# The place of one weight sum in VectorE's order, in a kernel of cosine attention and eight experts

## The chip, the cores and the metric

The kernel runs on one core of one Trainium2 chip. The metric is the device time of one execution in microseconds (us), as the median of several runs. A core has five engines with queues of their own: TensorE (PE in the profile, its weight loads PEld), VectorE (DVE), ScalarE (ACT), GpSimd (POOL) and SyncE (SP). Each works through its own queue in order. In this kernel POOL issues the loads of the inputs and weights, and SP issues the stores of the result and the saves and reloads of some sums.

## The reference

What is computed, cut to what matters:

```python
# attention: q, k, v are (8, 8, 576, 64); phi weights relu(x) with cos and sin of the position
kv = np.einsum('bhsf,bhsd->bhfd', k_p, v)
num = np.einsum('bhsf,bhfd->bhsd', q_p, kv)
den = np.einsum('bhsf,bhf->bhs', q_p, z)[..., None] + 1e-06
x = (num / den) as (4608, 512)

# experts: w1 is (8, 512, 1024), w2 is (8, 1024, 512)
P = np.exp(x @ w_gate - max)          # (4608, 8), then 8 rounds of row and column scaling
for e in range(8):
    h = np.maximum(x @ w1[e], 0.0)
    ye = h @ w2[e]
    out += P[:, e:e + 1] * ye
```

## The kernel before, in words

The kernel has two stages. The first, up to about 190 us, computes the attention into xT (fp16, held in SBUF), and beside it runs expert 0 on the token blocks that are already there. The second stage runs experts 1 to 7 on all 4608 tokens.

In the second stage every product of two matrices is cut into 2 x 2 blocks and done with seven block products instead of eight, after Strassen and Winograd. That takes sums of the operands' blocks ahead of the products and leaves sums of the results behind them.

- The tokens are two halves of 2304. A *unit* is 384 tokens of each half; there are six per expert, n = 0 to 5. Since the xT sums of a unit (S1, S2, S4) are the same for each expert, they are computed once, saved to DRAM by SP and read again for each expert (`x_again`).
- The first layer of a unit is four *groups*, i = 0 to 3 (`group`). A group multiplies with the banks h_ps, copied_ps (Y) and p_ps (Z). ScalarE writes part of the hidden values H through ReLU; VectorE writes the rest through `add_relu`, L600, one fused instruction that adds a saved partial result to the bank p_ps and applies ReLU. There is one bank p_ps, so the next product in it waits for L600. The last product of a group and its add are put off into the next group (`late`).
- The second layer works on pairs of 128 tokens (`Pair.step`, products P1 to P7). Its products go into the three banks rows_ps and into copied_ps, its sums of H are L678, and its accumulations into the result acc_lo and acc_hi are L666. The steps of a unit's pairs are queued in `stream` and woven by `pair_fill` between the first layer's products of the following unit.
- The sums of the weights are done on VectorE in place or into small tiles. `w1_sums` makes those of the first layer for one group (L583 to L586). `w2_first` makes the first of the second layer (L724): it overwrites the upper right block b12 of w2 by b12 - b11. The others (V2, V3, V4, at L689, L690 and L698) are made in the step P1 or P7 of the expert's first pair.
- The weights of expert e + 1 go into the buffer that expert e - 1 leaves (wA and wB in turn). POOL issues the load of w1 when unit 0 of expert e has been written out in the program, and that of w2 behind unit 2 (`load_w1`, `load_w2`, L116 and L122). A load is held until the last reader of the old weights is done.

In the program text, `w2_first(w_next)` is called once ahead of the loop over experts for expert 1, and then in unit 5 of each expert but the last, behind group 0, for the next expert. `w1_sums` for the next expert follow behind groups 1 to 3.

The order on an engine is not always that of the text. A scheduler places the instructions at compile time: in its own model of the time, each engine takes, of the instructions that are ready, the one that stands earliest in the text. An instruction that is ready while the engine would be idle can so stand far ahead of its place in the text. In the first stage, the kernel forbids that by the class `InOrder`, which ties each instruction to the one before it on its engine by an edge without a semaphore ("written order"). In the second stage only TensorE keeps that wrapper (`te`); `ve` and `se` are replaced by the bare engines, and VectorE's and ScalarE's orders are the scheduler's.

Of the kernel before, what the change touches and what calls it, by code (L numbers as in the profile page):

```python
# [14 lines left out]
ALU = mybir.AluOpType  # L15
# [10 lines left out]
def kernel(  # L26
# [10 lines left out]
    nc = tc.nc  # L37
# [41 lines left out]

    P_tok = const.tile([P, NG, E], FP32, name="P_tok")  # L80

    class InOrder:

        def __init__(self, engine):
# [3 lines left out]
        def __getattr__(self, name):  # L88
            def call(*args, **kwargs):
                i = getattr(self.engine, name)(*args, **kwargs)  # L90
                if self.last is not None:
                    tc.add_manual_dep(
                        i.ins,
                        self.last.ins.name,
                        mybir.DependencyInfo(
                            mybir.DependencyClass.NoSync, mybir.DependencyReason.DATA
                        ),
                        reason="written order",
                    )
                self.last = i  # L100
                return i

            return call
# [66 lines left out]
    with ExitStack() as p1:  # L170
# [15 lines left out]
        def load(b, hk):  # L186
# [22 lines left out]
            out=ident[:], in_=ones_sq[:], pattern=[[-1, P]], compare_op=ALU.is_equal,  # L209
# [6 lines left out]
        for hk in range(HK):  # L216
# [5 lines left out]
            out=wrap[:], in0=gidx[:], scalar1=float(S), scalar2=None, op0=ALU.is_ge  # L222
# [3 lines left out]
            out=sval[:], in0=wrap[:], scalar=-float(S), in1=gidx[:],  # L226
# [21 lines left out]
        with nc.allow_low_precision("sums of zeros and ones"):  # L248
            ve.tensor_reduce(
                out=lo[:], in_=rows[:, :, 1, :], axis=AX.XY, op=ALU.add, negate=True  # L250
# [3 lines left out]
                out=sel[:], in0=rows[:, 0:3, 0, :], in1=rows[:, 0:3, 1, :], op=ALU.add  # L254
            )
        ve.tensor_copy(
            out=spread.rearrange("p j hk hh d -> p (j hk hh) d"),
# [332 lines left out]
    def product(ps, lhs, rhs, start):  # L590

        for kh in range(KH):
# [2 lines left out]
                start=(start and kh == 0), stop=(kh == KH - 1), skip_group_check=True,  # L595
            )

    def add_relu(out, ps, t):

        nc.vector._custom_dve(  # L600
            TENSOR_ADD_SAT, out=out, in0=ps[:, 0:TU], in1=t[:], s0=FP32_MAX, s1=0.0
        )

# [7 lines left out]
    def group(hT, tw, xs, n, i, fill):  # L611
# [21 lines left out]
        fill()  # L633
        product(Z, T3, x_part(1, 0, n), True)
        add_relu(h22, Z, u4)
        fill()
        product(X, b22, s4, False)
# [3 lines left out]
        def last():  # L641
            product(Z, T4, x_part(1, 1, n), False)
            add_relu(h21, Z, u2)
# [77 lines left out]

    def w2_first(w):
        b11, b12 = w[1][:, 0:FH, 0:DH], w[1][:, 0:FH, DH:Dm]
        nc.vector.tensor_tensor(out=b12, in0=b12, in1=b11, op=ALU.subtract)  # L724

    def mark(bank):

# [116 lines left out]

    mark(Y[:])
    w2_first(w_next)
    for e in range(1, E):
        w = w_next
        for n in range(NU):
# [5 lines left out]
            for i in range(FH):  # L855
                group(hT, tws[i], xs, n, i, start_fill if e == 1 and n == 0 else pair_fill)
                if i == 1:

                    xs_next = x_tiles()
                    m = (n + 1) % NU  # L860
                    if e == 1 and m:
                        for _ in x_sums(m, xs_next):
                            pass
                    elif not (e == E - 1 and m == 0):
                        x_again(m, xs_next)

                if e > 1 and n == 0 and i == 0:
                    tws[FH - 1] = w1_sums(w, FH - 1)
                if e + 1 < E and n == NU - 1:
                    if i:  # L870
                        tws[i - 1] = w1_sums(w_next, i - 1)
                    else:
                        w2_first(w_next)
# [48 lines left out]
```

## Time and profile before

| | |
|---|---|
| median of 3 runs | 1050.51 us (1050.51 to 1052.1) |
| time of the profiled execution | 1050.02 us |
| its span, first to last instruction | 1048.3 us |
| mean granted TensorE clock | 0.988 |
| PE busy | 987.3 us, 94% |
| DVE busy | 838.9 us, 80% |
| ACT busy | 555.0 us, 53% |
| POOL busy | 129.6 us, 12% |

How to read it: busy time is that of the engine's own instructions. The table of waits puts each idle time of an engine down to what ended it. The chain is the sequence of work that ended last, followed back from the end. A row of a timeline gives the start and the duration in us, the engine, the line, the operation, what is written and what is read, and in brackets the idle time before it with what ended it. An "x4" at the end means that four like instructions are merged in the row. Line 90 is the helper through which instructions in written order are recorded. A window gives the busy time of each engine within a stretch and, behind POOL, the granted TensorE clock (1.00 is full speed). Names such as S_10585 and hs_10725 are tiles with a buffer number.

### The profile page before, as it was taken

To read this page: it belongs to the slowest core of one execution; us is meant where nothing else is said; L and a number is where in the kernel's file an instruction comes from. 1 tells how busy PE (TensorE), PEld (TensorE's weight loads), DVE (VectorE), ACT (ScalarE), POOL (GpSimd) and SP (SyncE) were. 2 spreads that over 40 slices of the span, in tenths; PEclk is the share of its full clock that TensorE was granted. 3 is DMA by queue.
4 is the path that set the end of the run, shared out by engine and by line. 5 is a ranking of instruction groups with operands and counts; after the bars stand their busy time and mean duration, and the time that the engine had idled before them with its cause. 6 is when DMAs were issued, how large, how long until landed. Compare 5 with 4: busy or idle time off the path is not lost.

```text
span 1048.3 us, 20469 instructions
## 1 busy us (share of the span) xinstructions
PE 987.3 (94%) x7914; PEld 684.5 (65%) x7914; DVE 838.9 (80%) x1898; ACT 555.0 (53%) x1244; POOL 129.6 (12%) x160
## 2 busy tenths in 40 slices
PE   4899999889999989998999989998999899999997
PEld 3455554345777757775777767775777667777775
DVE  6788777568999867886889778887879778888787
ACT  4666665345555545554555545554555445555551
POOL 7623200008950000000000000000000000000000
PEclk9999999999999999999999999999999989999999
DMA  9966501523102321033013311033013311013445
GB/s 166 202 87 90 82 4 46 81 41 69 41 23 63 63 48 46 24 83 67 24 35 74 62 31 41 24 86 64 23 46 63 64 38 32 24 46 94 127 91 122
DMA packets 52530, 66.49 MB, mean 63 GB/s; under 512 B 5584, under 2 KB 44240, under 8 KB 52432
## 3 DMA queue, kind: packets, MB, share of 16 engines
q0 software_dynamic: 28000, 30.94, 19.2%
q1 hardware_dynamic: 24352, 34.11, 11.8%
q8 instruction: 62, 1.02, 0.4%
q14 instruction: 36, 0.29, 0.1%
q10 hardware_dynamic: 80, 0.13, 0.1%
HBM read 83.12 MB, written 12.98 MB: 92 GB/s over the span
## 4 chain that ended last, share of the span: by engine, by line
PE 71%; issue 12%; DVE 8%; DMA 7%; ACT 1%; POOL 1%; POOLq 0%; DVEq 0%
PE rows_ps L90 25%; PE h_ps L90 20%; PE copied_ps L90 8%; PE p_ps L90 8%; DMA w2e<-in_moe_w_dram 6%; PE y_ps L90 5%; PE small_ps L90 4%; DVE acc_lo L666 1%; DVE H L600 1%; DVE k_p L90 1%; DVE acc_hi L666 1%; DMA k_ld<-in_k_dram 1%; DVE q_p L90 1%; DVE den L90 0%; DVE v_aug L90 0%
## 5 line engine op out<-in xcount | busy, mean ns | idle before, releaser
L666 DVE SCALAR_TENSOR_TENSOR acc_lo<-rows_ps,P_tok,acc_lo 128x512 f32<-128x512 f32 (+1 forms) x322 | 205.0, 642 | 82.4 <-PE rows_ps L90 82.4
L90 PEld LDWEIGHTS <-H 128*128 128x128 f16 x2080 | 204.3, 98 | 86.7 <-issue 4.8
L90 PEld LDWEIGHTS <-w1e 128*128 128x128 f16 x1632 | 156.8, 98 | 58.9 <-issue 5.8
L90 PE MATMUL h_ps<-xT,w1e 128*128 128x384 f16 (+1 forms) x624 | 156.3, 353 | 0.0
L638 ACT ACTIVATE H<-h_ps 128x384 f16<-128x384 f32 x168 | 82.7, 492 | 112.8 <-PE h_ps L90 112.8
L619 ACT COPY copied_ps<-h_ps 128x384 f32<-128x384 f32 x168 | 79.0, 470 | 41.8 <-PE h_ps L90 41.7
L629 ACT ACTIVATE H<-copied_ps 128x384 f16<-128x384 f32 x168 | 82.9, 493 | 24.7 <-PE copied_ps L90 24.6
L90 PE MATMUL rows_ps<-w2e,H 128*128 128x256 f16 (+1 forms) x568 | 91.9, 286 | 0.0
L90 PE MATMUL copied_ps<-xT,w1e 128*128 128x384 f16 x336 | 83.9, 332 | 0.0
L90 PE MATMUL copied_ps<-w2e,H 128*128 128x256 f16 x504 | 76.0, 274 | 0.0
L116 POOL DMA_DIRECT2D w1e<-in_moe_w_dram x11 | 8.3, 758 | 483.2 <-DVE T_3_7782 L583 89.4
L666 DVE SCALAR_TENSOR_TENSOR acc_lo<-copied_ps,P_tok,acc_lo 128x256 f32<-128x256 f32 x126 | 60.5, 480 | 1.8 <-PE copied_ps L90 1.3
L666 DVE SCALAR_TENSOR_TENSOR acc_hi<-rows_ps,P_tok,acc_hi 128x512 f32<-128x512 f32 x56 | 41.9, 749 | 19.8 <-PE rows_ps L90 19.0
L692 ACT COPY copied_ps<-rows_ps 128x256 f32<-128x256 f32 x126 | 45.2, 359 | 19.2 <-PE rows_ps L90 19.2
L90 PE MATMUL y_ps<-w2e,hT 128*128 128x512 f16 x224 | 54.3, 380 | 0.0
L783 POOL TENSOR_SCALAR acc_lo<-acc_lo,P_tok 128x512 f32<-128x512 f32 x32 | 53.9, 1701 | 0.5 <-DVE P_tok L759 0.5
L678 DVE TENSOR_TENSOR H<-H 128x512 f16<-128x512 f16 x126 | 53.4, 423 | 0.0
L90 ACT ACTIVATE hT<-h_ps 128x512 f16<-128x512 f32 x56 | 33.7, 602 | 17.6 <-PE h_ps L90 17.3
L90 PE MATMUL small_ps<-ident,q_p 128*128 128x128 f16 x288 | 27.4, 229 | 12.8 <-DVE q_p L90 9.0
L90 DVE TENSOR_TENSOR xT<-small_ps,rb 128x384 f16<-128x384 f32 x64 | 26.3, 453 | 16.1 <-ACT rb L90 14.9
L90 PEld LDWEIGHTS <-hT 128*128 128x128 f16 x224 | 19.5, 98 | 25.9 <-issue 6.2
L90 PEld LDWEIGHTS <-q_p 128*128 128x128 f16 x288 | 20.2, 102 | 24.6 <-DVE q_p L90 11.5
(2429 smaller groups left out, 2035.2 us busy)
## 6 DMA issues: line engine op xcount, KB each, us to landing
out_dram<-acc_lo SPq DMA_DIRECT2D x64, 128.0 KB, 2.4
w1e<-in_moe_w_dram POOLq DMA_DIRECT2D x7, 1024.0 KB, 8.9
w2e<-in_moe_w_dram POOLq DMA_DIRECT2D x7, 1024.0 KB, 9.6
q_ld<-in_q_dram POOLq DMA_DIRECT2D x32, 144.0 KB, 4.4
k_ld<-in_k_dram POOLq DMA_DIRECT2D x32, 144.0 KB, 4.6
v_ld<-in_v_dram POOLq DMA_DIRECT2D x32, 144.0 KB, 4.9
w1e<-in_moe_w_dram POOLq DMA_DIRECT2D x4, 256.0 KB, 7.2
w2e<-in_moe_w_dram POOLq DMA_DIRECT2D x4, 256.0 KB, 6.9
```

What stands on the lines that cost most here:

```text
L90: i = getattr(self.engine, name)(*args, **kwargs)
L116: nc.gpsimd.dma_start(out=w[0][:, :, f0:f1], in_=view[:, :, f0:f1])
L600: nc.vector._custom_dve(TENSOR_ADD_SAT, out=out, in0=ps[:, 0:TU], in1=t[:], s0=FP32_MAX, s1=0.0)
L619: nc.scalar.copy(out=Y[:, 0:TU], in_=X[:, 0:TU])
L629: nc.scalar.activation(out=h11, in_=Y[:, 0:TU], func=AF.Relu)
L638: nc.scalar.activation(out=h12, in_=X[:, 0:TU], func=AF.Relu)
L666: nc.vector.scalar_tensor_tensor(out=a, in0=rows, scalar=P_tok[:, g, self.e : self.e + 1], in1=a, op0=ALU.mult, op1=ALU.add,)
L678: nc.vector.tensor_tensor(out=out_, in0=in0, in1=in1, op=op)
L692: nc.scalar.copy(out=self.W, in_=self.U)
L783: nc.gpsimd.tensor_scalar(out=acc(g), in0=acc(g), scalar1=P_tok[:, g, 0:1], scalar2=None, op0=ALU.mult,)
```

## The change

A helper `not_before(earlier, i)` is taken out of `InOrder`: it adds the edge without a semaphore from an instruction `i` to an earlier one, if there is one. `add_relu` notes its last instruction in `latest`. `w2_first` ties its sum to that instruction. At its calls within the loop, `latest` is the add of the product Z in group 0 of unit 5 of the current expert (h22). At the call ahead of the loop no add_relu has been written, `latest` is None, and no edge is added.

```diff
+    def not_before(earlier, i):
+
+        if earlier is not None:
+            tc.add_manual_dep(
+                i.ins,
+                earlier.ins.name,
+                mybir.DependencyInfo(mybir.DependencyClass.NoSync, mybir.DependencyReason.DATA),
+                reason="written order",
+            )
+
     class InOrder:
...
                 i = getattr(self.engine, name)(*args, **kwargs)
-                if self.last is not None:
-                    tc.add_manual_dep(
-                        i.ins,
-                        self.last.ins.name,
-                        mybir.DependencyInfo(
-                            mybir.DependencyClass.NoSync, mybir.DependencyReason.DATA
-                        ),
-                        reason="written order",
-                    )
+                not_before(self.last, i)
                 self.last = i
                 return i
...
+    latest = None
+
     def add_relu(out, ps, t):
 
-        nc.vector._custom_dve(
+        nonlocal latest
+        latest = nc.vector._custom_dve(
             TENSOR_ADD_SAT, out=out, in0=ps[:, 0:TU], in1=t[:], s0=FP32_MAX, s1=0.0
         )
...
     def w2_first(w):
         b11, b12 = w[1][:, 0:FH, 0:DH], w[1][:, 0:FH, DH:Dm]
-        nc.vector.tensor_tensor(out=b12, in0=b12, in1=b11, op=ALU.subtract)
+        not_before(latest, nc.vector.tensor_tensor(out=b12, in0=b12, in1=b11, op=ALU.subtract))
```

## The prediction

> **What bounds the kernel now.** I read the page's busy shares and chain first, then the table of waits, then the timelines of VectorE and TensorE around one wait, then windows cut at the units of the second stage.
>
> ```profile
> PE 987.3 (94%) x7914; PEld 684.5 (65%) x7914; DVE 838.9 (80%) x1898; ACT 555.0 (53%) x1244; POOL 129.6 (12%) x160
> PE 71%; issue 12%; DVE 8%; DMA 7%; ACT 1%; POOL 1%; POOLq 0%; DVEq 0%
> w2e<-in_moe_w_dram POOLq DMA_DIRECT2D x7, 1024.0 KB, 9.6
> ```
>
> TensorE (PE) is busy for 94% of the span, so it is the bound nearly everywhere. Yet 7% of the chain is DMA, and that is worth following, since a weight load of 9.6 us should hide in a stage of hundreds of us. The chain in order of time, and the table of waits, say where it doesn't:
>
> ```profile
> 827.35 9.70 DMA w2e<-in_moe_w_dram
> 837.68 0.74 DVE acc_lo L666
> 838.94 0.80 PE p_ps L90 x2
> ```
>
> ```profile
> DVE w2e L724 <- DMA w2e<-in_moe_w_dram: 26.2, 7, 4.6
> PE p_ps L90 <- DVE H L600: 25.6, 13, 4.8
> ```
>
> L724 is the first sum of the next expert's second layer weights. VectorE (DVE) stood still for it 7 times, 26.2 us in all, and TensorE stood still for DVE's adds L600 for 25.6 us, almost the same sum. The timelines of DVE, TensorE and POOL show that it is one event:
>
> ```profile
> 832.01 0.42 DVE L678 TENSOR_TENSOR H<-H 128x512 f16<-128x512 f16 x1
> 837.07 0.69 DVE L724 TENSOR_TENSOR w2e<-w2e 128x1024 f16<-128x1024 f16 x1 [4.64 <-DMA w2e<-in_moe_w_dram]
> 837.68 0.74 DVE L666 SCALAR_TENSOR_TENSOR acc_lo<-rows_ps,P_tok,acc_lo 128x512 f32<-128x512 f32 x1
> 838.34 0.55 DVE L600 CUSTOM_DVE_ANT_0 H<-p_ps,u_10851 128x384 f16<-128x384 f32 x1
> ```
>
> ```profile
> 833.52 0.60 PE L90 MATMUL rows_ps<-w2e,H 128*128 128x256 f16 x4
> 838.94 0.80 PE L90 MATMUL p_ps<-xT,T_2_10458 128*128 128x384 f16 x2 [4.82 <-DVE H L600]
> 839.54 1.06 PE L90 MATMUL rows_ps<-V_10766,H 128*128 128x256 f16 x4
> ```
>
> ```profile
> 827.35 0.89 POOL L122 DMA_DIRECT2D w2e<-in_moe_w_dram  x1 [25.44 <-PE rows_ps L90]
> ```
>
> POOL issues the load at 827.35. DVE reaches L724 at 832.4, less than 5 us later, and waits until 837.07. Behind it in DVE's queue stand an accumulation and the add L600 that empties the bank p_ps; TensorE's next product needs that bank and waits 4.82 us. Then TensorE runs slowly: four matmuls of 256 columns take 1.06 us where they took 0.60. The windows give the whole price. Each of the first six rows is the unit of 384 tokens per half in which a load lands, for experts 1 to 6; the seventh is the same unit of expert 7, which loads nothing for a successor.
>
> ```profile
> core 0: us, PE busy (x) PEld busy (x) DVE busy (x) ACT busy (x) POOL busy (x), PEclk, DMA share, GB/s
> 244.45:262.75 18.30, 17.40 (x129) 12.49 (x128) 15.69 (x34) 10.15 (x23) 18.30 (x12) 1.00 0.43 88
> 355.26:380.31 25.05, 20.27 (x143) 14.32 (x141) 17.03 (x37) 10.33 (x23) 0.89 (x1) 0.93 0.37 67
> 471.71:496.80 25.09, 20.18 (x143) 14.32 (x140) 17.12 (x37) 10.33 (x23) 0.89 (x1) 0.93 0.37 65
> 588.21:613.10 24.89, 19.96 (x143) 14.24 (x141) 17.12 (x37) 10.33 (x23) 0.89 (x1) 0.93 0.37 67
> 704.50:729.09 24.59, 20.02 (x143) 14.24 (x141) 17.19 (x37) 10.32 (x23) 0.89 (x1) 0.93 0.38 69
> 820.49:847.03 26.54, 21.47 (x142) 14.78 (x140) 17.17 (x37) 10.33 (x23) 0.89 (x1) 0.87 0.36 64
> 938.44:957.13 18.69, 18.44 (x143) 13.68 (x140) 16.43 (x36) 10.23 (x23) 0.00 (x0) 1.00 0.26 70
> 838.94:844.66 5.72, 5.72 (x23) 3.19 (x23) 2.38 (x5) 1.45 (x3) 0.00 (x0) 0.50 0.16 41
> ```
>
> The last row is the stretch behind the wait: granted clock 0.50 for 5.72 us, so 2.86 us are lost there. 4.82 of idle and 2.86 of slow clock make 7.68, and the unit is 26.54 - 18.69 = 7.85 longer than the clean one. That agrees, so I price each wait by its unit's excess and not by DVE's 4.6 us.
>
> **The change, part by part.** *The wait goes from experts 2 to 6.* The edge puts L724 behind `latest`, the last add_relu written when w2_first is called: group 0 of unit 5 of the same expert. Gain, each unit against 18.69: 6.36 + 6.40 + 6.20 + 5.90 + 7.85 = 32.71. Expert 7's unit is a fair measure, since it runs the same products, pair steps and weight sums, and only lacks load and L724. What is late next in that unit: its remaining 0.41 over a plain unit of 18.28 (below), which I leave in.
>
> *Expert 1's unit.* Here DVE waited less and TensorE only 0.60:
>
> ```profile
> 251.86 0.69 DVE L724 TENSOR_TENSOR w2e<-w2e 128x1024 f16<-128x1024 f16 x1 [1.54 <-DMA w2e<-in_moe_w_dram]
> 253.07 0.48 PE L90 MATMUL p_ps<-xT,T_1_3602 128*128 128x384 f16 x2 [0.60 <-DVE H L600]
> ```
>
> Gain between 0 (the next units are short of DVE time anyway) and 0.60; I take 0.3. The call ahead of the loop finds `latest` empty, so the seventh wait stays:
>
> ```profile
> 204.35 0.69 DVE L724 TENSOR_TENSOR w2e<-w2e 128x1024 f16<-128x1024 f16 x1 [2.58 <-DMA w2e<-in_moe_w_dram]
> ```
>
> *L724 in its new place.* It costs DVE 837.68 - 837.07 = 0.61 us of its queue, once per expert, six times. It is not new work, but it moves from the unit above to unit 5, where the sums of the next expert's first layer weights already stand. The rows: unit 5 of expert 6, a unit of expert 1 that is as full, and an ordinary one; then DVE's adds and TensorE's product around the place.
>
> ```profile
> 901.88:920.16 18.28, 18.28 (x142) 13.70 (x140) 17.79 (x48) 10.23 (x23) 0.00 (x0) 1.00 0.12 35
> 281.19:300.23 19.04, 18.52 (x142) 13.69 (x140) 17.82 (x38) 10.23 (x23) 19.04 (x13) 1.00 0.09 32
> 802.21:820.49 18.28, 18.28 (x142) 13.68 (x140) 14.96 (x34) 10.23 (x23) 0.00 (x0) 1.00 0.46 90
> ```
>
> ```profile
> 904.35 0.56 DVE L600 CUSTOM_DVE_ANT_0 H<-p_ps,u_11628 128x384 f16<-128x384 f32 x1
> 914.24 0.55 DVE L600 CUSTOM_DVE_ANT_0 H<-p_ps,u_11748 128x384 f16<-128x384 f32 x1
> ```
>
> ```profile
> 914.94 0.49 PE L90 MATMUL p_ps<-xT,T_2_10458 128*128 128x384 f16 x2
> ```
>
> L724 will start near 904.8 in this expert, right behind the add of 904.35. DVE is busy for 17.79 of this unit's 18.28 us, so I let its 0.61 be handed on in full. The add of 914.24 would end at 914.24 + 0.61 + 0.55 = 915.40, and TensorE wants its bank at 914.94: about 0.45 of waiting. Bounds: 0 per expert, since unit 5 itself now runs at 18.28 with DVE at 17.79, and 17.79 + 0.61 = 18.40 is only 0.12 over, while the unit behind it is as light as the ordinary one (14.96); and 0.76, from the full unit of expert 1 (19.04 - 18.28 with DVE at 17.82). The nearest row is unit 5 itself, so I go below the middle: 0.2, six times 1.2, with 0 and 4.6 as ends. Queued behind L724 there are accumulations, adds L600 and the weight sums of the next expert.
>
> *Does anything wait for L724 itself?* Its result is first read by the sum of the next expert's first pair,
>
> ```profile
> 939.41 0.68 DVE L689 TENSOR_TENSOR V_12084<-w2e 128x1024 f16<-128x1024 f16 x1
> ```
>
> 34 us behind the new place; and the load landed at 837, 67 us ahead of it. So no new wait on either side: cost 0, covered by these margins. If the cover were gone, the price would be the present wait again.
>
> *Queues.* L724 issues no DMA. POOL's load of w2 waits for the last reader of the old buffer, on TensorE, and stays where that puts it; SP's reloads of x don't depend on it. TensorE's order is written out and unchanged. The helper not_before replaces the same code in InOrder and costs nothing: the same edges. What can move is the scheduler's choice on DVE around the two places; I count that in the ends.
>
> *Sum.* 32.7 + 0.3 - 1.2 = 31.8 us. The profiled execution took 1050.02 (span 1048.3), so it would be 1018.2. The median of the runs is 1050.51, 0.5 above it: forecast 1018.7. About 0.2%, 2 us, is what a measurement here can tell from no change.
>
> **Rivals.**
> *Full units turn dearer.* The scheduler's new order lets unit 5 lose up to the 0.76 of expert 1's full unit: 1018.7 - 1.2 + 4.6 = 1022.1, and a little more with other swaps on DVE. For it: DVE at 17.79 of 18.28. Against: the light unit behind.
>
> *The clock drops in unit 5.* If short waits there made TensorE lose its clock once per expert, at the 2.86 that one slow stretch costs, six of them are 17.2: 1036. Against it: the wait of 0.60 in expert 1 was followed by a product of 0.48 us at full speed, and that unit's granted clock is 1.00, as in the full unit of 19.04. [...]
>
> *Only part of the wait goes.* Something else that depends on the load is drawn early into the free place, and half of the price stays: 1018.7 + 16 = 1035. Against: the other DVE readers of the new weights all stand behind L724 by their data.
>
> *It does nothing.* If `latest` stood early in DVE's order, or the edge were not kept, L724 would stay at 837 and the time at 1050.5. Against: an add of unit 5 can't run ahead of its own product, and that add is the row at 904.35.
>
> *Slower.* DVE's lag in unit 5 grows instead of draining: L724's 0.61 delays the add that frees p_ps, TensorE comes late with its products, and DVE's next instructions wait for these. It decides from 33.0 / 6 = 5.5 us lost per expert, a wait as long as the one removed with its slow clock; at 7 us per expert, 1050.5 - 33.0 + 42 = 1059.5. Against: nine times the instruction's own time, beside a unit with over 3 us of DVE idle.
>
> **How the numbers follow.** Forecast (waits gone, unit 5 hidden or nearly) 72%; dearer full units 13%; clock 4%; part of the wait 4%; nothing 3%; slower 3%; better than my ends 1%. Faster by over 0.2%: 72 + 13 + 4 + 4 + 1 = 94%; within 3%; slower 3%. Low end: 1050.5 - 32.7 - 0.6 = 1017.2, less 1.5 for expert 1's three units, of which the 19.04 is 0.76 over the floor, and for differences between executions: 1015.5. High end: 1022.1 and as much for swaps, 1023.5. Outside lie the clock, the part, nothing and slower, 14%, and the few per cent beyond the low end.
>
> **What would show it.** L724 should stand in unit 5 of each expert but the last, some 70 us later than now, with no idle time before it; DVE's 26.2 us for the load should shrink to the one wait ahead of the loop, about 2.6 us; TensorE's 25.6 for L600 to some 2; the five long units should read 18.3 to 18.8 at a granted clock of 1.00, and DMA should leave the chain there. Units 5 should read 18.3 to 18.7. A unit 5 above 19, a clock under 1.00 in it, or another instruction in front of a DMA wait would show me wrong; wrong on the sum would be a slow stretch that the removed wait did not cause.

## The result, and the profile after

| | before | changed |
|---|---|---|
| median | 1050.80 us (1050.51 to 1052.1, 4 runs) | 1018.13 us (1017.22 to 1019.35, 4 runs) |
| ratio to before | | 0.9688, 95% interval 0.9671 to 0.9704 |
| profiled execution, its span | 1050.02, 1048.3 | 1019.35, 1017.6 |
| granted TensorE clock | 0.988 | 0.996 |

32.7 us went, 31.8 were forecast. In the changed kernel lines lie a few further down: the sum is L729, the fused add L605, the accumulation L671, the helper L100. First the page of the changed kernel, its engines and the shares of its chain:

```profile
PE 981.0 (96%) x7914; PEld 682.1 (67%) x7914; DVE 838.2 (82%) x1898; ACT 553.5 (54%) x1244; POOL 128.1 (13%) x160
PE 88%; DVE 8%; DMA 1%; ACT 1%; issue 1%; POOL 0%; POOLq 0%; DVEq 0%; ACTq 0%
```

DMA was 7% of the chain and "issue" 12%; both are 1% now, and PE has taken their place, 88% for 71%. The table of waits has the same two entries as before, smaller:

```profile
DVE w2e L729 <- DMA w2e<-in_moe_w_dram: 2.2, 1, 2.2
PE p_ps L100 <- DVE H L605: 2.8, 8, 1.0
```

26.2 us in 7 waits became 2.2 in one, the one ahead of the loop, and TensorE's 25.6 became 2.8. In the timeline the sum of expert 7 stands in unit 5 without idle time before it (start, duration, engine, line):

```profile
873.58 0.56 DVE L605 CUSTOM_DVE_ANT_0 H<-p_ps,u_11628 128x384 f16<-128x384 f32 x1
874.71 0.68 DVE L729 TENSOR_TENSOR w2e<-w2e 128x1024 f16<-128x1024 f16 x1
883.73 0.54 DVE L605 CUSTOM_DVE_ANT_0 H<-p_ps,u_11748 128x384 f16<-128x384 f32 x1
```

Windows of the changed kernel: the five units in which a load lands, experts 2 to 6, and then unit 5 of experts 1, 2 and 6.

```profile
core 0: us, PE busy (x) PEld busy (x) DVE busy (x) ACT busy (x) POOL busy (x), PEclk, DMA share, GB/s
356.64:375.32 18.68, 18.43 (x142) 13.69 (x140) 16.42 (x36) 10.21 (x23) 0.89 (x1) 1.00 0.50 89
466.87:485.56 18.69, 18.44 (x143) 13.68 (x141) 16.43 (x36) 10.21 (x23) 0.88 (x1) 1.00 0.51 89
577.11:595.79 18.68, 18.43 (x142) 13.69 (x140) 16.42 (x36) 10.21 (x23) 0.89 (x1) 1.00 0.51 91
687.35:706.03 18.68, 18.43 (x142) 13.68 (x140) 16.42 (x36) 10.21 (x23) 0.89 (x1) 1.00 0.50 90
797.59:816.27 18.68, 18.43 (x143) 13.68 (x140) 16.42 (x36) 10.21 (x23) 0.89 (x1) 1.00 0.51 89
```

```profile
319.92:338.36 18.44, 18.44 (x142) 13.69 (x140) 18.26 (x49) 10.21 (x23) 0.81 (x1) 1.00 0.12 35
430.16:448.60 18.44, 18.44 (x143) 13.68 (x141) 18.25 (x49) 10.21 (x23) 0.75 (x1) 1.00 0.12 33
871.10:889.54 18.44, 18.44 (x142) 13.68 (x140) 18.25 (x49) 10.21 (x23) 0.00 (x0) 1.00 0.11 33
```

The five long units now take what expert 7's clean one took before, at a clock of 1.00, while the loads still land in them (DMA share 0.50). Unit 5 pays: DVE 17.79 to 18.25, the unit 18.28 to 18.44. The ledger of the two spans, each unit cut at its first product that reads one of the sums S:

| stretch | change, us |
|---|---|
| up to expert 1's unit 0 (222.39 before, 223.45 after) | +1.06 |
| expert 1, units 1 to 4 (18.30 18.44 19.04 18.47 before; 17.60 19.45 18.90 18.46 after) | +0.16 |
| unit 1 of experts 2 to 6 (126.16 before, 93.41 after) | -32.75 |
| unit 5 of experts 1 to 6 (6 x 0.16) | +0.96 |
| sum; the spans differ by 30.7 | -30.57 |

The medians differ by 32.7, but the two traced executions only by 30.7 (1050.02 and 1019.35): that of the changed kernel is the slowest of its four, and that of the kernel before is shorter than its four runs in the table. These 2.0 lie between executions, and the ledger can't place them; that its 32.75 for the five units equals the difference of the medians is chance.

### The profile page after: what moved, and what is told of

It reads as the page before. It is cut to its first block, busy times and chain, and to the rows that moved or that the text cites. A ratio compares the mean times of both kernels' runs of the same rounds, so it can differ in the third digit from the quotient of the medians.

```text
span 1017.6 us, 20469 instructions
## 1 busy us (share of the span) xinstructions
PE 981.0 (96%) x7914; PEld 682.1 (67%) x7914; DVE 838.2 (82%) x1898; ACT 553.5 (54%) x1244; POOL 128.1 (13%) x160
## 4 chain that ended last, share of the span: by engine, by line
PE 88%; DVE 8%; DMA 1%; ACT 1%; issue 1%; POOL 0%; POOLq 0%; DVEq 0%; ACTq 0%
PE rows_ps L100 32%; PE h_ps L100 25%; PE p_ps L100 11%; PE copied_ps L100 11%; PE y_ps L100 5%; PE small_ps L100 5%; DVE k_p L100 1%; DMA w1e<-in_moe_w_dram 1%; DVE H L605 1%; DVE acc_hi L671 1%; DMA k_ld<-in_k_dram 1%; DVE acc_lo L671 1%; DVE q_p L100 1%; DVE den L100 0%; DVE q_pT L100 0%
## 5 line engine op out<-in xcount | busy, mean ns | idle before, releaser
L671 DVE SCALAR_TENSOR_TENSOR acc_lo<-rows_ps,P_tok,acc_lo 128x512 f32<-128x512 f32 (+1 forms) x322 | 204.9, 640 | 76.1 <-PE rows_ps L100 75.9
L100 PEld LDWEIGHTS <-H 128*128 128x128 f16 x2080 | 203.3, 98 | 85.6 <-issue 4.2
L100 PEld LDWEIGHTS <-w1e 128*128 128x128 f16 x1632 | 156.3, 98 | 57.9 <-issue 4.7
L100 PE MATMUL h_ps<-xT,w1e 128*128 128x384 f16 (+1 forms) x624 | 157.4, 355 | 0.0
L100 PE MATMUL rows_ps<-w2e,H 128*128 128x256 f16 (+1 forms) x568 | 93.2, 289 | 0.0
L100 PE MATMUL copied_ps<-xT,w1e 128*128 128x384 f16 x336 | 82.1, 326 | 0.0
L100 PE MATMUL copied_ps<-w2e,H 128*128 128x256 f16 x504 | 75.5, 272 | 0.0
L671 DVE SCALAR_TENSOR_TENSOR acc_lo<-copied_ps,P_tok,acc_lo 128x256 f32<-128x256 f32 x126 | 60.1, 477 | 0.8 <-PE p_ps L100 0.4
L671 DVE SCALAR_TENSOR_TENSOR acc_hi<-rows_ps,P_tok,acc_hi 128x512 f32<-128x512 f32 x56 | 41.7, 745 | 19.1 <-PE rows_ps L100 19.0
L100 PE MATMUL y_ps<-w2e,hT 128*128 128x512 f16 x224 | 54.3, 380 | 0.0
L100 ACT ACTIVATE hT<-h_ps 128x512 f16<-128x512 f32 x56 | 33.6, 599 | 18.7 <-PE h_ps L100 18.2
L100 DVE TENSOR_TENSOR xT<-small_ps,rb 128x384 f16<-128x384 f32 x64 | 26.3, 452 | 16.1 <-ACT rb L100 14.9
L100 PE MATMUL small_ps<-ident,q_p 128*128 128x128 f16 x288 | 27.9, 232 | 11.9 <-DVE q_p L100 8.9
L100 PEld LDWEIGHTS <-hT 128*128 128x128 f16 x224 | 19.5, 98 | 25.8 <-issue 6.2
L100 PEld LDWEIGHTS <-q_p 128*128 128x128 f16 x288 | 20.8, 103 | 23.9 <-DVE q_p L100 11.0
```

The lines of the kernel that those rows point to most:

```text
L671: nc.vector.scalar_tensor_tensor(out=a, in0=rows, scalar=P_tok[:, g, self.e : self.e + 1], in1=a, op0=ALU.mult, op1=ALU.add,)
```

## The experiments

The theory: the price was the wait for the load, passed on by the one bank p_ps, and behind a long wait TensorE's clock (0.50 for 5.72 us behind the 4.82 of expert 6); the place of L724 matters only in that it must come after the landing, and in that it takes 0.6 us from the unit where it runs. The rivals: the place or the load's traffic costs time by itself; the price goes with VectorE's wait; scheduling out of the text's order is dear in general.

**A shorter wait at the old place.** The kernel before, with two loads of 512 KB for one of 1 MB; L724 reads only rows of the first.

```diff
-                load_w2(w_next, e + 1, 1)
+                load_w2(w_next, e + 1, 2)
```

> The kernel before (no hold), but each load of the next expert's second layer weights is issued in two pieces of 512 KB, and L724 reads only the rows of the first piece. L724 stands at the same place in VectorE's order but for two instructions. Theory (the price is the wait for the transfer at that place): loads of 256 KB landed in 6.9 us and of 1024 KB in 9.6 us, so the first piece should land about 2 us earlier, the wait falls from 4.5 to 2 to 3 us, TensorE's idle time in the five units to under 3 us, and the unit's length from 25 us to 21 to 22; if the clock only drops behind waits of over 4 us, the granted clock of these units stays 1.00. Time 1028 to 1040 us. Rival (the place itself or the memory traffic of the load costs the time, not the wait): the units stay at 24.5 us and over, 1048 to 1052 us.

1024.3 us, 0.9732 (0.9716 to 0.9749). The five units of this kernel, and its wait for expert 7's load:

```profile
355.96:376.33 20.37, 18.59 (x142) 13.68 (x140) 16.93 (x37) 10.21 (x23) 1.48 (x2) 1.00 0.45 80
467.72:487.65 19.93, 18.60 (x142) 13.69 (x140) 16.94 (x37) 10.21 (x23) 1.48 (x2) 1.00 0.46 85
579.04:599.10 20.06, 18.60 (x142) 13.68 (x140) 16.95 (x37) 10.21 (x23) 1.48 (x2) 1.00 0.47 85
690.49:710.29 19.80, 18.60 (x143) 13.67 (x141) 17.00 (x37) 10.21 (x23) 1.48 (x2) 1.00 0.47 85
801.68:821.66 19.98, 18.60 (x142) 13.68 (x140) 16.94 (x37) 10.21 (x23) 1.48 (x2) 1.00 0.46 85
```

```profile
814.24 0.69 DVE L724 TENSOR_TENSOR w2e<-w2e 128x1024 f16<-128x1024 f16 x1 [1.42 <-DMA w2e<-in_moe_w_dram]
```

Without any hold, and with as many bytes loaded, four fifths of the gain are there by the units (26.0 of 32.7). VectorE even comes to L724 a little earlier in the unit, by two instructions (11.14 us into it for 11.94). So neither the traffic nor the place by itself is the cause. I had the wait at 2 to 3 us; it was 1.42 here, so the units and the time came out below what I wrote.

**A move of four instructions.** The edge goes to an add of unit 1 instead of unit 5; VectorE's order is otherwise that of before.

```diff
+        adds.append(nc.vector._custom_dve(TENSOR_ADD_SAT, ...))      # each add_relu, in text order
...
+                        w2_first(w_next, adds[2 * (((e - 1) * NU + 1) * FH + 2) + 0])
```

> L724 is moved by only four instructions of VectorE from its place before: behind the first add of group 2 in unit 1 (and so in front of that group's second add), instead of some 70 us. No other instruction of VectorE changes its place. In the clean unit of expert 7 that place lies at 952.2 where the load would land at 955.0, so L724 would still wait 2.8 us. Theory (the bank p_ps passes on only what the next product cannot absorb, and a short wait leaves the clock alone): the held add would end near 956.2 where TensorE wants the bank at 954.5, so 1.7 us of idle per unit, units of 20.4 us, clock 1.00, time 1024 to 1028 us. Rival (price in proportion to VectorE's wait): 2.8 / 4.5 of 6.5 us, 4.0 per unit, time 1036 to 1040 us. Rival (any wait of over 1 us costs the clock too): 3.5 to 4.5 per unit, clock near 0.93, time 1034 to 1040 us.

1025.55 us, 0.9746 (0.9731 to 0.976). L724 of expert 7, still waiting, and the product behind it:

```profile
819.72 0.69 DVE L728 TENSOR_TENSOR w2e<-w2e 128x1024 f16<-128x1024 f16 x1 [3.07 <-DMA w2e<-in_moe_w_dram]
```

```profile
820.93 0.48 PE L100 MATMUL p_ps<-xT,T 128*128 128x384 f16 x2 [1.83 <-DVE H L604]
```

VectorE waits 3.07, TensorE only 1.83, and its product runs at full speed (0.48). The units read 20.10, 21.01, 20.63, 20.01 and 20.68 (1.8 on average over 18.69), all at clock 1.00. That is the theory's 1.7 and not the 4.0 of a price in proportion to VectorE's wait.

**A move of eight instructions.** As the last, with `+ 2` for `+ 0`: behind the first add of group 3.

> L724 is moved by eight instructions of VectorE, behind the first add of group 3 in unit 1, which in the clean unit of expert 7 lies at 955.7, after the landing at 955.0. Theory: no wait, or under 0.5 us; the five units read 18.7 to 19.2, unit 5 goes back from 18.44 to 18.28, and the whole gain of the change is there with a move of a few us: 1016.5 to 1020 us. Rival (what helps is the far place beside unit 5, or fewer instructions in unit 1): units of unit 1 stay over 20 us, time over 1026 us.

1017.92 us, 0.9674 (0.966 to 0.9688). The unit of expert 6 with the load, and its unit 5:

```profile
796.41:815.09 18.68, 18.43 (x142) 13.69 (x140) 17.02 (x37) 10.21 (x23) 0.89 (x1) 1.00 0.52 89
869.92:888.21 18.29, 18.29 (x143) 13.69 (x141) 17.80 (x48) 10.21 (x23) 0.00 (x0) 1.00 0.12 33
```

All five units read 18.68 or 18.69. The whole gain is there with a move of a few us, and unit 5 is back at its old length: the distance of 70 us in the change has no part in it.

**From which idle time the clock drops.** The kernel before, with loads of 768 and 256 KB.

```diff
-            f0, f1 = i * FT // cuts, (i + 1) * FT // cuts
+        ends = (0, 6, FT) ...      # the next experts' w2 in rows 0 to 5 and 6 to 7 of 8
```

> The kernel before (no hold), its w2 loads issued as a piece of 768 KB and one of 256 KB; L724 waits for the first piece, at nearly its old place in VectorE's order. It asks from which idle time on TensorE's clock drops: idle times up to 2.2 us kept the clock (two pieces of 512 KB, hold by 4 places), those of 4.3 to 4.8 us in the kernel before lost it. The first piece should land 1 us before the whole load did, so TensorE should idle for 2.5 to 3.7 us per unit. [...] If 2.5 us already costs it: units of 23 to 24, clock 0.93 to 0.96, time 1038 to 1046 us. A mixture over the five units would say that the moment counts beside the length.

1039.1 us, 0.9897 (0.9881 to 0.9914). The five units show both cases side by side; below them, TensorE's first products behind the wait in the first and the third:

```profile
355.20:378.61 23.41, 20.15 (x142) 14.31 (x140) 16.94 (x37) 10.31 (x23) 1.52 (x2) 0.93 0.40 73
470.00:493.62 23.62, 20.27 (x142) 14.33 (x140) 16.98 (x37) 10.31 (x23) 1.52 (x2) 0.93 0.40 70
585.02:606.65 21.63, 18.59 (x142) 13.69 (x140) 16.94 (x37) 10.21 (x23) 1.52 (x2) 1.00 0.42 77
698.04:719.70 21.66, 18.59 (x142) 13.69 (x140) 17.00 (x37) 10.21 (x23) 1.52 (x2) 1.00 0.44 77
811.10:835.58 24.48, 20.26 (x142) 14.41 (x140) 16.94 (x37) 10.31 (x23) 1.52 (x2) 0.93 0.36 68
```

```profile
371.84 0.80 PE L90 MATMUL p_ps<-xT,T 128*128 128x384 f16 x2 [3.01 <-DVE H L600]
372.43 1.06 PE L90 MATMUL rows_ps<-V,H 128*128 128x256 f16 x4
...
601.43 0.48 PE L90 MATMUL p_ps<-xT,T 128*128 128x384 f16 x2 [2.79 <-DVE H L600]
601.76 0.60 PE L90 MATMUL rows_ps<-V,H 128*128 128x256 f16 x4
```

An idle time of 3.01 is followed by slow products, one of 2.79 is not: the mixture named in the expectation. The time lies in the range that I gave for a lost clock, although two of the five units kept theirs. The 25 waits in these units of five kernels follow (the last two rows are the kernel before without POOL's scaling, from an experiment below): TensorE's idle time against what its unit is longer than 18.69:

| kernel | TensorE idle, us | unit's excess, us | clock of the unit |
|---|---|---|---|
| two loads of 512 KB | 0.95 to 1.53 | 1.11 to 1.68 | 1.00 |
| hold by four | 1.17 to 2.16 | 1.32 to 2.32 | 1.00 |
| 768 + 256 KB | 2.79, 2.82 | 2.94, 2.97 | 1.00 |
| 768 + 256 KB | 3.01, 3.10, 3.97 | 4.72, 4.93, 5.79 | 0.93 |
| before | 4.32, 4.53, 4.66, 4.68 | 5.90, 6.36, 6.40, 6.20 | 0.93 |
| before, expert 6 | 4.82 | 7.85 | 0.87 |
| before, without the scaling | 4.37, 4.45, 4.66, 5.29 | 6.20, 6.27, 6.42, 7.05 | 0.93 |
| before, without the scaling, expert 4 | 5.07 | 8.09 | 0.87 |

In these units a wait of up to 2.82 costs itself and 0.15; from 3.01 on, 1.5 to 1.8 more, twice 3.0. The dearer two are not the longest: 4.82 and 5.07 cost 3.0 more, 5.29 cost 1.8 more.

The length alone doesn't decide, though. Near 200 us TensorE also waits for about 3 us: 3.20 in the kernel before, 3.07 in the changed one, 3.08 with the move of four and 3.18 with the move of eight. The two rows there come first from the kernel before, then from the kernel with the move of eight; the last two are from expert 1's unit 0 with all of VectorE in text order (below):

```profile
199.64 0.55 PE L90 MATMUL copied_ps<-t_3448,scale_row 1*128 1x8 f32 x2 [3.20 <-DVE t_3448 L753]
200.13 1.89 PE L90 MATMUL h_ps<-xT,w1e 128*128 128x512 f16 x4
...
200.10 0.38 PE L100 MATMUL copied_ps<-t,scale_row 1*128 1x8 f32 x2 [3.18 <-DVE t L757]
200.42 1.04 PE L100 MATMUL h_ps<-xT,w1e 128*128 128x512 f16 x4
...
237.85 0.20 PE L90 MATMUL copied_ps<-colp,ones_col 128*1 128x8 f32 x2 [2.72 <-DVE colp L90]
237.98 0.82 PE L90 MATMUL h_ps<-S,w1e 128*128 128x384 f16 x2
```

Behind 3.20 the products are slow (1.89), behind 3.18 they are not (1.04), and behind 2.72 they are again (0.82 for 0.49). Behind the 3.07 of the changed kernel they are slow as well (1.89), and the kernel with the move of four kept its clock there behind 3.08 (its granted clock over the whole execution is 1.00). So between 2.72 and 3.18 both outcomes are on record, and no run here gives a limit.

**A lighter unit for L724.** As the change, but the call stands in unit 3.

```diff
-                    else:
-                        w2_first(w_next)
+                if e + 1 < E and n == 3 and i == 0:
+                    w2_first(w_next)
```

> As the change, but the call stands in unit 3 and the edge goes to unit 3's first add, so that L724 runs in a unit where VectorE is busy for 15 of 18.28 us instead of 17.8. Theory (the new place costs what unit 5 is short of): unit 5 falls from 18.44 to 18.28, unit 3 stays at 18.28, no wait for the load; 0.16 for each of six experts, about 1 us less than the change: 1016 to 1019 us, which one comparison of medians can hardly tell from the change but the units can. Rival (the 0.16 comes from elsewhere, as from the order of the other instructions): unit 5 stays at 18.44.

1016.91 us, 0.9664 (0.9649 to 0.9678). Units 3 and 5 of expert 6:

```profile
832.42:850.70 18.28, 18.28 (x143) 13.68 (x141) 15.47 (x34) 10.21 (x23) 0.00 (x0) 1.00 0.11 33
868.98:887.25 18.27, 18.27 (x142) 13.69 (x140) 17.79 (x48) 10.21 (x23) 0.00 (x0) 1.00 0.11 35
```

With DVE at 15.47, L724 is free there, and unit 5 has its 0.16 back. The change and this version were then run side by side.

> The changed kernel once more, on the same chip and in the same rounds as the hold in unit 3: 0.966 to 0.971 of the kernel before.

> The hold in unit 3, beside the change in the same rounds. Theory (unit 5 is relieved of 0.16 us for each of six experts, and expert 1's units 3 and 4 by 0.36 in its first trace): 1 to 1.5 us less than the change. Rival: no difference beyond 0.5 us.

The change: 1019.4 us, 0.9707 (0.9694 to 0.9721). In unit 3: 1017.01 us, 0.9688 (0.9675 to 0.9701). The two intervals still overlap a little, and the 2.4 us between the medians are more than the 1 to 1.5 that I gave. The two traced executions differ by 2.7 us, and 1.27 of these are from the units: 0.86 in experts 2 to 7 and 0.41 in expert 1. The other 1.42 lie ahead of expert 1's unit 0, where the two kernels do not differ by design, and where the traces shown here start between 217.79 (the text order below) and 223.48; I don't count those as a gain of the version.

**Why expert 1 gained nothing.** POOL's scaling of expert 0's part of the result (36 instructions) is left out of expert 1's units, so that part of the result is unscaled; VectorE's order is the same, instruction by instruction, as in the kernel before and the changed one.

```diff
-            if e == 1:
-                gate(n)
```

> The kernel before without POOL's scaling of expert 0's part in the units of expert 1 (32 instructions of 1.7 us, L783), so that part of the result is unscaled; VectorE's order is the same instruction by instruction. It asks why expert 1's first units gained 0.70 by the change and gave 1.01 back in the next. Theory (VectorE's fp16 sums take longer while POOL works on SBUF, 0.7 to 1.0 us instead of 0.42 to 0.56, and which of them are hit depends on the time): expert 1's units 2 and 3 fall from 18.44 and 19.04 to 18.3 to 18.5, and no sum of H there takes over 0.6 us. Rival (those units are short of VectorE's time by their x sums alone): 18.44 and 19.04 stay. Time 1048 to 1051 us.

> The same removal from the changed kernel. Theory: expert 1's units 2 and 3 fall from 19.45 and 18.90 to 18.3 to 18.5, so that the 0.6 of unit 1 is no longer given back: 1.5 us less than the change, 1015.5 to 1018 us. Rival: 19.45 and 18.90 stay, 1017 to 1019 us.

1050.86 us, 0.9992 (0.998 to 1.0004), from the kernel before, and 1016.83 us, 0.968 (0.9665 to 0.9694), from the changed one. Units 1 and 2 of expert 1 in the changed kernel, and then in it without POOL's scaling:

```profile
245.51:263.11 17.60, 17.30 (x129) 12.48 (x128) 15.02 (x33) 10.12 (x23) 17.60 (x11) 1.00 0.44 91
263.11:282.56 19.45, 18.44 (x143) 13.67 (x141) 18.19 (x38) 10.21 (x23) 19.45 (x14) 1.00 0.09 32
```

```profile
244.19:261.64 17.45, 17.15 (x129) 12.49 (x128) 14.38 (x33) 10.12 (x23) 0.00 (x0) 1.00 0.45 91
261.64:279.92 18.28, 18.28 (x143) 13.66 (x141) 16.37 (x37) 10.21 (x23) 0.00 (x0) 1.00 0.09 34
```

One sum of H in that unit, in the kernel before and the changed one, both with POOL at work, and without it:

```profile
265.49 0.43 DVE L678 TENSOR_TENSOR hs_4060<-H,hs_4059 128x512 f16<-128x512 f16 x1
```

```profile
266.75 0.71 DVE L683 TENSOR_TENSOR hs_4060<-H,hs_4059 128x512 f16<-128x512 f16 x1
```

```profile
264.38 0.42 DVE L683 TENSOR_TENSOR hs<-H,hs 128x512 f16<-128x512 f16 x1
```

The same instruction takes 0.43 or 0.71 beside POOL's scaling, and 0.42 without it. Of the single sums of H in expert 1's units 1 to 3, the longest took 0.90 before and 0.96 in the changed kernel, and at most 0.43 without the scaling. Unit 2's DVE time falls by 1.82 (18.19 to 16.37), and the unit is a plain one. Without POOL's scaling, units 2 and 3 read 18.29 and 18.28 in the kernel before and 18.28 and 18.27 in the changed one, so the gain of unit 1 (18.36 to 17.45) is not given back in the next unit. Why some sums take longer beside POOL's scaling is not shown: most took 0.41 to 0.43 although POOL's record there has no gap (busy for all 19.45 us of unit 2). One more thing stays open: unit 5 of expert 1 reads 18.80 in the changed kernel without the scaling (18.44 with it, 18.28 in the kernel before either way). So 0.52 of unit 1's gain is lost there after all, and only 0.16 of it is L724's price.

**All of VectorE in text order.**

```diff
+    ve2 = ve                    # keeps the written order of the first stage
     ve, se = nc.vector, nc.scalar
...
-        nc.vector.tensor_tensor(...)
+        ve2.tensor_tensor(...)  # and so for every sum, add and accumulation of the second stage
```

> Not one sum but all of VectorE's instructions of the second stage are held in the order of the program text (no instruction may be drawn early), with nothing else changed. Theory (only the one instruction that depends on a load stood wrongly, the other early places fill VectorE's gaps): the waits for the load go, the five units lose their 25 us, but sums and adds in text order make TensorE wait more often, units of 18.4 to 20: time 1020 to 1060 us. Rival (the scheduler's early places cost in general): faster than the change, under 1016 us.

1031.66 us, 0.9818 (0.9804 to 0.9833). The load's waits go here too: unit 1 of expert 6 reads 18.93 and unit 5 18.77, each a little over the change's 18.68 and 18.44. Expert 1 pays most, 127.88 us for 114.91 from its unit 0 to the end of unit 5, though it starts 5.66 earlier (217.79 for 223.45). So taken together the scheduler's early places were worth having, but for the one instruction that waits for a load; which of them matter in expert 1 was not tested.

## Why the prediction was right, by its own steps

- *The five waits*: 32.71 forecast, 32.75 measured. To price a wait by its unit's excess over a clean unit, with the slow clock in it, was the step that carried it: the idle times alone are 23.0 (4.53 + 4.66 + 4.68 + 4.32 + 4.82).
- *Expert 1's unit*: a gain of 0.3 was forecast, 0.16 was lost. The term had the wrong sign. Unit 1 gained 0.70, above my end of 0.60, and unit 2 lost 1.01. I had called the next units short of DVE time, but had no end below nothing. What I left out is that DVE's sums can take longer beside POOL's scaling (the one shown above took 0.43 before, 0.71 in the changed kernel and 0.42 without the scaling); without it the four units gain 0.93 (73.21 to 72.28), and unit 5 then takes 0.52 of that back.
- *Unit 5*: 1.2 forecast, 0.96 measured, 0.16 for each expert. The mechanism is the one worked out, the add that empties p_ps in group 2, but I had handed on all of 0.61, which gave 0.45; the 0.2 was a choice between my bounds and not that working. In unit time that add starts at 883.73 - 871.10 = 12.63, and before at 914.24 - 901.88 = 12.36: 0.27 was handed on. The other 0.34 went because one sum of H, which ran ahead of that add before (913.25), now runs behind it (884.59); such a swap I had counted only in the ends. Its product begins at 884.33 by the timeline of the changed kernel, 13.23 into the unit, 0.17 later than before (13.06).
- *No new wait on either side of L724, nor in the queues*: held. The one wait left is that ahead of the loop, 2.2.
- *The clock*: no drop in unit 5, which reads 1.00 at 18.44 us, as the rows had said. The one wait that the prediction shows ahead of slow products is 4.82; the same trace has them behind 3.20 at 199.64, and in these runs drops occur from 2.72 on.
- *Not in the sum*: the start of expert 1's unit 0 is 1.06 later in the changed trace. It lay at 223.48 when the same kernel was run again, and between 222.06 and 223.24 in the kernels with other holds, with split loads or without the scaling. Of the 1.06, 1.00 is there within the first 53 us (VectorE's row of xT at 52.39 stands at 53.39), 150 us ahead of the first L724, and without the scaling it is the kernel before that is late (53.28) and the changed one that is early (52.52). So it doesn't come from the change; its cause stays open.
- *The total*: the three terms make 31.63 in the traces, 31.8 forecast. The later start took 1.06 from that, and the executions differ by 2.0 the other way, so that 1018.7 came within 0.6 of the median is in part luck.
- *A reading*: VectorE reached L724 5.08 us behind the issue (832.43 - 827.35), not under 5. Nothing rests on it.

That something else would wait for the load, that unit 5 would lose 0.76, and that nothing would change are all excluded by the rows above.

## What to carry to other kernels

When an engine stands still for a DMA, look for an instruction that stands in its queue too close behind the issue of the transfer it reads; a move of eight instructions, about 5 us, brought the whole gain, and splitting the transfer so that the first piece covers what is read brought four fifths of it in these units. Price such a wait by the length of its stretch against a clean one, since what hides part of it (here the bank: 3.07 us of VectorE's wait left TensorE idle for 1.83) and what adds to it (here the clock: 3.03 us behind an idle time of 4.82) both show there. Put the moved work where its engine has time: 0.6 us cost 0.16 beside DVE at 17.79 of 18.28 and nothing beside DVE at 14.96.

## What the hardware showed that was not expected

- In the units looked at, TensorE's clock stayed at 1.00 behind idle times of up to 2.82 us and dropped behind those of 3.01 and more; elsewhere in the traces of these runs it stayed behind 3.08 and 3.18 and dropped behind 2.72. So length alone doesn't decide. Of the 13 drops in those units two cost 3.0 us and the others 1.5 to 1.8. What decides either is not shown by any run here.
- With the load of expert 7 split in two pieces of 512 KB, L724 started 5.71 us behind the issue (814.24 - 808.53) instead of 9.72 (837.07 - 827.35), 4.0 sooner, where I had worked out 2 from the times to landing of loads of 256 KB (6.9 us) and 1 MB (9.6 us).
- Two-input fp16 sums on VectorE took up to 2.3 times as long beside POOL's scaling (0.96 for 0.42 us).
